# Attention's opening, the first expert's routing and the place of the second expert's counts in a kernel of attention and two MoE layers

## The chip, the cores and the metric

The kernel runs on one core of one Trainium2 chip. The metric is the device time of one execution in microseconds (us). TensorE (PE in the rows; PEld is its weight load), VectorE (DVE), ScalarE (ACT), GpSimd (POOL) and SyncE (SP, which issues most DMAs) each work off an instruction queue of their own, in order.

## What is computed

Attention with 4 sink positions and a window of 128, then an MoE layer in which each token goes to its best expert, then an MoE layer in which each expert takes at most 384 tokens, by the order of all logits.

```python
def _attn_ref(q, k, v, n_sink, window):             # (4, 8, 768, 64)
    scores = scale * np.matmul(q, k.transpose(0, 1, 3, 2))
    keep = is_sink | in_window                       # 4 sinks, window 128
    scores = np.where(keep, scores, -1000000000.0)
    a = np.exp(scores - np.max(scores, axis=-1, keepdims=True))
    a = a / (np.sum(a, axis=-1, keepdims=True) + 1e-09)
    return np.matmul(a, v).astype(np.float32)

def _moe_ref(x, modality_id, w_gate, modality_bias, w1, w2):   # x (3072, 512), 8 experts, 1024 hidden
    logits = x @ w_gate + modality_bias[modality_id]
    e_idx = np.argmax(logits, axis=1)
    ...
        h = np.maximum(x[mask] @ w1[e], 0.0)
        out[mask] = gate_w[mask, None] * (h @ w2[e])

def _moe2_ref(x, w_gate, w1, w2):
    cap = N // E                                     # 384
    flat = (x @ w_gate).flatten()
    for idx in np.argsort(-flat):
        tok, e = (int(idx) // E, int(idx) % E)
        if assigned[tok] >= 0 or counts[e] >= cap:
            continue
        assigned[tok] = e
        counts[e] += 1
    ...
        h = np.maximum(x[mask] @ w1[e], 0.0)
        out[mask] = h @ w2[e]
```

## The kernel before

**Attention** (0 to 200 us) goes through 48 groups `k` of two units each, three groups to a pair of heads. Each group's scores (`qk_mm`, L306) go through masks and maximum on VectorE (L317 to L325), the exponential on ScalarE (L335), a transpose on TensorE (L343), a copy on ScalarE (L348), a select on GpSimd (L354, L359) and the product with v (L378, a group later). The sinks have a path of their own: `sinkpack` (L387, L388, GpSimd), `sinktr` (L392), and `rows` (L411, L413), which multiplies with `bd`, a table that `init` (L257 to L285) builds in the first twenty steps from the sink values `vst` and `vsx` (both loaded), with dots `px<-wgp,vst` on TensorE (L264), their split into high and low part (`vsh`), and products into `bd` on ScalarE, GpSimd and VectorE. `warm` (L225) issues matmuls on zeros, 14 ahead of the loop and 7, 6, 5, 4, 3, 2 behind, which produce nothing. Other work (tables, routing of the first MoE, gathers of its first two tiles) stands in a list `bg`, of which the loop pops two steps a group.

**First MoE.** `Gate.after_batch` routes each of the four batches in steps `v1` to `v4` (L564 to L597); `v3b` (L588, L590) counts with matmuls of the one-hot table `oh`. Batch 2's steps are popped in the first FFN steps.

**FFN.** `Ffn.run` lists steps (an expert's quarter of the hidden width each). Each operand is split into a high and a low part, so a product is three matmuls: `ph<-xh/xl,w1h/w1l` (L930) and `y<-w2h/w2l,hh/hl` (L873). The low parts of the weights are made on VectorE or GpSimd (L845, L826). The rows of the next expert are gathered by GpSimd (L1744, three indirect DMAs of 128 rows), and `xprep` (L740 to L742) transposes them in four lots of 3 at fixed places in steps 6 and 7 of the expert ahead.

**Second MoE's routing** (`Route.steps`) finds each expert's threshold by iterations: a comparison `cmp` of 128x1792 on VectorE, thirteen count matmuls `rt<-OH,cmp` (L1560), two small operations, a matmul `rt<-gg,ones` (L1813), a maximum, and the next bound. After the last iteration `A` marks the expert's tokens, and `compact_steps` (L1387 to L1419) turns it into row numbers `idx`: a sum, a rank, and 28 matmuls `rc<-ft,ohb` (L1419). The first expert's iterations run with nothing beside them but `warm` (L749, by the numbers in `WT`); the others' run in between the FFN's matmuls. A planner's clock sets their place: a step is taken when the estimated clock of TensorE has reached the estimated end of VectorE's work plus a constant, `CM[0]`, `CM[1]`, `CM[2]` for the counts of the first, the second and all later experts (`yield clk.dve + CM[...]`).

Of the kernel before, what the change touches and what calls it, by code (L numbers as in the profile page):

```python
# [22 lines left out]
NSINK = 4  # L23
# [17 lines left out]
NSL = 128 * NSUB  # L41

C_ID, C_CAUS, C_M0, C_M1, C_TRI, C_IOTA, C_IW, C_BD, C_P = 0, 128, 256, 384, 512, 640, 768, 832, 840
C_W = 848


def host_consts():
# [24 lines left out]
def load_consts(nc, g, cpool, cst):  # L72
# [25 lines left out]
def late_consts(nc, g):  # L98
# [8 lines left out]
    def small():  # L107
        V.tensor_scalar(g.tcol[:, :, 0], g.iota[:, 0:NT], -1.0, float(NT - 1), op0=OP.mult, op1=OP.add)
        V.tensor_scalar(g.tcol[:, :, 1], bc(g.cst[:, C_P:C_P + 1], [128, NT]), -1.0, 128.0, op0=OP.mult, op1=OP.add)
        V.memset(g.tcr, 0.0)  # L110
# [5 lines left out]
        V.memset(g.o1, 1.0)  # L116
# [3 lines left out]
    return [small] + [(lambda t=t, c=c, o=o, w=w: fill(t, c, o, w))  # L120
                      for t, c, o, w in ((g.iob, 1.0, 0, 64), (g.iob, 1.0, 64, 64), (g.iou, 128.0, 0, 32), (g.iou, 128.0, 32, 32))]
# [62 lines left out]
def attention(ctx, tc, g, qT, kT, v4, vsT, vsR, wg, put_x, after_batch, bg, drain=True):  # L184
# [32 lines left out]
    load_pair(0)  # L217
    g.cst_load()
    load_pair(1)
    load_v(0)  # L220

    def warm(k):
        pz = ps.tile([128, 512], F32, name="po", bufs=2)
        for _ in range(k):
            nc.tensor.matmul(pz, g.wz[:, :128], g.wz, start=True, stop=True)  # L225

    warm(WARM)
    neg = one.tile([128, 128], F32, name="neg")
# [9 lines left out]
    nc.gpsimd.memset(rw[:, :, 128:144], 0.0)  # L238
    for s in range(2):
        o = slice(64 * s, 64 * s + 64)  # L240
        nc.sync.dma_start(rw[o, :, 128 + 8 * s:136 + 8 * s], wgv[o])
    bd = one.tile([96, B * NP, 2, 144], F32R, name="bd")
    psk = []
    for i in range(4):
        t = one.tile([128, 3, 8, NSINK], F32R, name=f"psk{i}")
        nc.gpsimd.memset(t.bitcast(F32), 0.0)
        psk.append(t)
    nc.gpsimd.memset(bd[:, 0:4].bitcast(F32), 0.0)
    vsh = wk.tile([96, B * NP, 72], F32, name="vsh", bufs=1)
    msk = one.tile([128, 3, 128], I32, name="msk")  # L250
    for c in (0, 2, 4):
        scale_q(0, c)
    for i, c in ((1, C_M0), (2, C_M1), (0, C_CAUS)):
        nc.vector.tensor_copy(msk[:, i, :], g.cst[:, c:c + 128])

    def init(n):
        V = nc.vector  # L257
        if n == 0:
            g.cst_derive()
            V.tensor_copy(rw[:, :, 0:128], bc(g.ident[:, None, :], [128, NP, 128]))  # L260
        if n in (2, 4):
            g.pw = ps.tile([96, B * NP, 8], F32, name="px")
        for p in {2: range(4), 4: range(4, 10), 5: range(10, 16)}.get(n, ()):
            nc.tensor.matmul(g.pw[:, p, :], vst[:, p, :], wgp[:, p % NP, :], start=True, stop=True)  # L264
        if n in (3, 6):
            r = slice(0, 4) if n == 3 else slice(4, 16)
            V.tensor_copy(vsx[:, r, 64:72], g.pw[:, r])
            V.tensor_copy(vsh[:, r].bitcast(F32R), vsx[:, r])
        if n in (4, 7):
            r = slice(0, 4) if n == 4 else slice(4, 16)  # L270
            V.tensor_tensor(vsh[64:96, r].bitcast(F32R), vsx[64:96, r], vsh[64:96, r], op=OP.subtract)
        k = n - 5 if n < 9 else (4 + (n - 9) // 2 if (n - 9) % 2 == 0 else 16)
        if 0 <= k < 16:
            c, m = divmod(k, 4)
            blk, hd = divmod(m, 2)
            mk = g.cst[:96, C_BD + m:C_BD + m + 1]
# [1829 lines left out]
```

## Time and profile before

| what | us |
|---|---|
| median of three runs (lowest, highest) | 882.87 (882.37, 883.36) |
| the profiled execution | 881.1 |
| its span, first to last instruction | 879.4 |
| attention | 0 to 200 |
| first MoE | 200 to 490 |
| its tail and the second MoE's first routing | 480 to 535 |
| second MoE's FFN, with the other experts' routing | 535 to 879 |

All rows below are of the profiled execution. Their times count from the start of the span. In a timeline row the first number is the start, the second the duration, then the engine, the line of the kernel, the operation, what it writes and reads, the shape and a count; in brackets the idle time of the engine ahead of it and what ended that. Neighbouring operations of a kind share a row.

### The profile page before, as it was taken

What the parts mean: (1) busy time and instruction counts of PE and PEld (TensorE: products, weight loads), DVE (VectorE), ACT (ScalarE), POOL (GpSimd) and SP (SyncE); (2) the same over time, 40 slices, a digit from 0 to 9 for tenths busy, and PEclk for the clock granted to TensorE, in tenths of its full rate; (3) what the DMA queues carried; (4) which work ended last, traced back from release to release, by engine and by line L of the source; (5) the groups of instructions that cost most, each with busy time, mean ns of one, the idle gap of its engine ahead of it and who ended that gap; (6) DMA issues with size and microseconds to landing.
All of it is one profiled execution on the core that took longest, in us unless ns stands there. A gap on an engine that the chain in (4) does not pass through costs nothing.

```text
span 879.4 us, 15309 instructions
## 1 busy us (share of the span) xinstructions
PE 835.4 (95%) x5071; PEld 664.3 (76%) x5071; DVE 597.0 (68%) x1737; ACT 387.1 (44%) x1093; POOL 354.9 (40%) x555
## 2 busy tenths in 40 slices
PE   8789999998999999999999987899999999999997
PEld 4556666676888888888888646788888878889996
DVE  3868787866659696969794467767778775753320
ACT  3677777764343434243342204243334333445431
POOL 2776757573420202010000006435464637375561
PEclk9999999999999999999999998998999999999999
DMA  8344555467463434444358133424435424336201
GB/s 252 111 144 144 138 157 150 101 220 285 56 190 108 154 118 157 130 156 133 108 156 279 64 104 130 153 78 145 166 122 181 161 91 142 119 134 226 96 37 40
DMA packets 69773, 123.90 MB, mean 141 GB/s; under 512 B 9651, under 2 KB 22453, under 8 KB 69558
## 3 DMA queue, kind: packets, MB, share of 16 engines
q1 hardware_dynamic: 62998, 103.41, 37.0%
q0 software_dynamic: 6688, 19.43, 7.0%
q8 instruction: 42, 0.69, 0.3%
q14 instruction: 45, 0.37, 0.2%
HBM read 103.11 MB, written 19.71 MB: 140 GB/s over the span
## 4 chain that ended last, share of the span: by engine, by line
PE 76%; DVE 9%; issue 5%; ACT 4%; POOL 2%; DMA 2%; SPq 1%; POOLq 0%; DVEq 0%; ACTq 0%
PE ph L930 27%; PE y L873 27%; PE sp L306 4%; PE po L378 3%; ACT P L335 2%; PE tr L740 2%; PE rt L1560 2%; PE pt L343 2%; PE px L413 1%; PE rc L1419 1%; DMA vsx<-in_vsR_dram 1%; DVE sc L150 1%; PE sp L392 1%; DMA xg<-xs,idx 1%; PE ph L1203 1%
## 5 line engine op out<-in xcount | busy, mean ns | idle before, releaser
L940 ACT ACTIVATE hh<-ph 128x384 fp32r<-128x384 f32 (+1 forms) x112 | 60.2, 538 | 276.7 <-PE ph L930 276.6
L930 PE MATMUL ph<-xh,w1h 128*128 128x384 f32 (+1 forms) x448 | 170.2, 380 | 0.0
L930 PE MATMUL ph<-xh,w1l 128*128 128x384 f32 (+1 forms) x448 | 162.5, 363 | 0.0
L930 PE MATMUL ph<-xl,w1h 128*128 128x384 f32 (+1 forms) x448 | 161.6, 363 | 0.0
L873 PE MATMUL y<-w2h,hh 128*128 128x512 f32 x384 | 155.8, 406 | 0.0
L873 PE MATMUL y<-w2h,hl 128*128 128x512 f32 x384 | 151.8, 395 | 0.0
L873 PE MATMUL y<-w2l,hh 128*128 128x512 f32 x384 | 151.7, 395 | 0.0
L941 DVE SCALAR_TENSOR_TENSOR hl<-ph,hh 128x384 fp32r<-128x384 f32 (+1 forms) x112 | 68.4, 611 | 113.8 <-ACT hh L940 112.5
L826 POOL TENSOR_TENSOR w2l<-w2r,w2h 128x512 fp32r<-128x512 f32 x64 | 89.0, 1399 | 63.9 <-ACT w2h L822 33.0
L1096 POOL DMA_INDIRECT xg<-xd,ent x26 | 29.3, 1126 | 190.1 <-DMA ent<-idtab 100.1
L1120 DVE SCALAR_TENSOR_TENSOR junk<-yr,wgb 128x512 f32<-128x512 f32 x160 | 103.0, 683 | 0.0
L930 PEld LDWEIGHTS ph<-xh,w1h 128*128 128x128 f32 x448 | 86.0, 192 | 10.0
L930 PEld LDWEIGHTS ph<-xh,w1l 128*128 128x128 f32 x448 | 85.7, 191 | 9.4
L930 PEld LDWEIGHTS ph<-xl,w1h 128*128 128x128 f32 x448 | 85.0, 190 | 7.8
L335 ACT ACTIVATE P<-sp,mx 128x132 f32<-128x132 f32 x192 | 69.2, 368 | 48.9 <-DVE mx L325 22.5
L873 PEld LDWEIGHTS y<-w2h,hl 128*128 128x128 f32 x384 | 72.9, 190 | 16.1
L873 PEld LDWEIGHTS y<-w2h,hh 128*128 128x128 f32 x384 | 73.3, 191 | 11.5
L873 PEld LDWEIGHTS y<-w2l,hh 128*128 128x128 f32 x384 | 73.1, 190 | 11.4
L306 PE MATMUL sp<-kr,qs 64*128 64x260 f32 (+1 forms) x384 | 58.4, 401 | 16.4 <-ACT P L335 16.3
L840 ACT ACTIVATE w1h<-w1r 128x512 fp32r<-128x512 f32 x112 | 69.7, 623 | 5.7 <-DMA w1r<-in_w_dram 3.4
L822 ACT ACTIVATE w2h<-w2r 128x512 fp32r<-128x512 f32 x112 | 69.6, 624 | 0.5 <-DMA w2r<-in_w_dram 0.5
L845 DVE TENSOR_TENSOR w1l<-w1r,w1h 128x512 fp32r<-128x512 f32 x80 | 63.4, 793 | 3.5 <-ACT w1h L840 3.5
(359 smaller groups left out, 1394.0 us busy)
## 6 DMA issues: line engine op xcount, KB each, us to landing
w1r<-in_w_dram SPq DMA_DIRECT2D x30, 1024.0 KB, 5.7
w2r<-in_w_dram SPq DMA_DIRECT2D x30, 1024.0 KB, 7.2
kr<-in_kT_dram SPq DMA_DIRECT2D x16, 396.0 KB, 4.5
qr<-in_qT_dram SPq DMA_DIRECT2D x16, 384.0 KB, 3.3
vr<-in_v_dram SPq DMA_DIRECT2D x16, 384.0 KB, 4.9
xd<-xb SPq DMA_DIRECT2D x16, 384.0 KB, 4.4
xs<-yr SPq DMA_DIRECT2D x24, 256.0 KB, 5.3
wgb<-in_wg2T_dram SPq DMA_DIRECT2D x1, 2048.0 KB, 12.0
```

The source lines that it names most:

```text
L306: nc.tensor.matmul(sp[:, hd, c0:260], qs[o:o + 64, 128 * i:128 * i + 128], kr[o:o + 64, k0:k0 + 260 - c0], start=True, stop=True)
L335: nc.scalar.activation(z.P[:, n % 2, hd, :], s.sp[:, hd, 128:260], AF.Exp, bias=s.mx[:, hd:hd + 1], accum_out=z.sm[:, n % 2, hd:hd + 1])
L822: nc.scalar.activation(ch[1][c][0], r[:, q, :], AF.Copy)
L826: eng.tensor_tensor(lo, r[:, q, :], h.bitcast(F32), op=OP.subtract)
L840: nc.scalar.activation(h, v, AF.Copy)
L845: eng.tensor_tensor(lo, v, h.bitcast(F32), op=OP.subtract)
L873: nc.tensor.matmul(o, l, r, start=(first and i == 0), stop=(end and i == 2))
L930: nc.tensor.matmul(ph, wp[:, c, :], xp_[:, c, 0:NTK], start=(d == 0 and i == 0), stop=(d == 3 and i == len(cut[d]) - 1))
L940: nc.scalar.activation(hh, ph, AF.Relu)
L941: nc.vector.scalar_tensor_tensor(hl, ph, 0.0, hh.bitcast(F32), op0=OP.max, op1=OP.subtract)
L1096: self.nc.gpsimd.indirect_dma_start(out=self.xg[j][:, a, :], out_offset=None, in_=self.G.xd[0:k, :], in_offset=bass.IndirectOffsetOnAxis(a ...
L1120: nc.vector.scalar_tensor_tensor(junk, yr[:, 0:DM], 1.0, wgb[:, e, :], op0=OP.mult, op1=OP.mult, accum_out=lg[:, e:e + 1])
```

## The change

**Opening.** The first pair's q and k are loaded in two pieces; the table of constants shrinks from 848 to 272 columns, as masks and the triangle are made on GpSimd and VectorE; `vst` is no longer loaded but built on GpSimd from a small table; `vsx` is loaded for four heads first, the other twelve behind the second pair; 9 warming matmuls stand ahead of the loop, and 7, 4, 3, 2 in the first four groups, behind the transposes; the sink dots go in fours to groups 1, 4, 6 and 8; the products into `bd` go to groups 2, 3 and every second group from 8 on; `bg` is popped from group 2 on; the clearing of `bd` goes.

**First MoE.** Only its first tile is gathered in attention's background; batch 2's steps are popped in attention's last groups, and its `v3b` gets the place rule that batch 3's had.

**Second MoE.** For the first expert the bound comes from a table `T` with one fused operation, and the comparison is split, 8 of 14 columns first, so that counts can start; `A` is made ahead of `cj` and `em`; `WT[2]` and `WT[3]` become 0 and 1 for the first expert (6 and 3 for the others, as before); a gather of 2 rows into the first expert's tile is issued at the start (`prime`); the first expert's transposes go block by block (`xfirst`). `CM[1]` goes from 0.7 to 2.0.

```diff
-WARM, WARM1 = 14, 8
+JC, NIT, FEW, IDLE = 64, 4, 2, (1, 2, 1)
+WARM, WARM1, WA = 9, 8, (7, 4, 3, 2)
-CM = 0.2, 0.7, 1.3
+CM = 0.2, 2.0, 1.3
-WT = 5, 2, 6, 3, 6, 2, 3, 16, 0, 2
+WT = 5, 2, (0, 6), (1, 3), 6, 2, 3, 16, 0, 2
...
+    raw[0] = wk.tile([128, S], F32, name="qr"), wk.tile([128, KW], F32, name="kr", bufs=3)
+    for qc, kc in ((slice(0, 256), slice(0, 2 * SEG)), (slice(256, S), slice(2 * SEG, KW))):
+        nc.sync.dma_start(raw[0][0][:, qc], qT[0, 0][:, qc])
+        nc.sync.dma_start(raw[0][1][:, kc], kT[0, 0][:, kc])
...
-    nc.sync.dma_start(vst, vsT)
-    nc.sync.dma_start(vsx[:, :, 0:64], vsR)
+    nc.sync.dma_start(vsx[:, 0:4, 0:64], vsR[:, 0:4])
+    load_v(0)
+    load_pair(1)
+    nc.sync.dma_start(vsx[:, 4:16, 0:64], vsR[:, 4:16])
+    P.memset(vst, 0.0)
...
+            P.tensor_scalar(v[:, :, a, s].rearrange("p (b z) s -> p b z s", z=3),
+                            bc(vsc[o, :, None, :], [64, B * NP, 3, NSINK]), 1.0, 1.0, op0=OP.mult, op1=OP.mult)
+    VC = {1: (0,), 4: (1,), 6: (2,), 8: (3,)}
...
-        v = [v1, v1b, v2, v2b, v3] + ([(RW, v3b)] if b == B - 1 else [nop, v3b]) + [v4]
+        v = [v1, v1b, v2, v2b, v3] + ([(RW, v3b)] if b > BE else [nop, v3b]) + [v4]
...
+        for a in range(A):
+            for d in range(4):
+                nc.tensor.transpose(p[d][:, 128 * a:128 * a + 128], xg[:, a, 128 * d:128 * d + 128], self.g.ident)
...
+                    if k == 0:
+                        if it > first:
+                            V.scalar_tensor_tensor(self.ub, bc(dd[:, 2, it - 1:it], [128, NR]), J, self.T, op0=OP.mult, op1=OP.add)
+                            self.against(V)
...
+                            V.tensor_scalar(self.T, S_, b1, dd[:, 1, it + 1:it + 2], op0=OP.subtract, op1=OP.mult)
...
-                    self.count(pn, range(HT + 1))
+                    self.count(pn, range(HT + 1), k == 0 and it > first)
```

TensorE in attention's opening, before: the sink dots of six heads stand between the scores of two groups.

```order
L306 MATMUL sp<-kr,qs 128x260 x2
L264 MATMUL px<-wgp,vst 96x8 x6
L343 MATMUL pt<-cst,P 128x128 x4
L378 MATMUL po<-lu,vr 64x256 x2
L306 MATMUL sp<-kr,qs 128x132 x2
L306 MATMUL sp<-kr,qs 128x260 x2
L392 MATMUL sp<-cst,psk_170 96x128
```

The same engine after the change, in group 1:

```order
L322 MATMUL sp<-kr,qs 128x260 x4
L359 MATMUL pt<-cst,P 128x128 x4
L273 MATMUL sp<-wgp,vst 96x8 x4
L220 LDWEIGHTS wz
L220 MATMUL px<-wz 128x512
```

The dots moved behind the transposes, four heads at a time, and into the bank of the scores.

TensorE at the seam of attention and the first MoE, before, where the last row matmuls are followed by the first transposes:

```order
L411 MATMUL px<-bd,skT 128x288
L413 MATMUL px<-rw,oT 128x144 x2
L740 MATMUL tr<-cst,xg 128x128 x4
L740 MATMUL ph<-cst,xg 128x128 x4
L740 MATMUL y_3258<-cst,xg 128x128 x4
```

After:

```order
L427 MATMUL px<-bd,skT 128x288
L429 MATMUL px<-rw,oT 128x144 x2
L615 LDWEIGHTS tri
L615 MATMUL px<-oh,tri 128x48
L617 LDWEIGHTS ones
L617 MATMUL px<-oh,ones 128x48
```

Batch 2's counts (one matmul with `tri`, six with `ones`) moved from the first FFN step to right behind the last rows; five more count matmuls and then the transposes follow.

TensorE in the second MoE, before, from the last of expert 1's 28 compaction matmuls (21 FFN matmuls stand between it and the first transposes `tr<-cst,xg`):

```order
L1419 MATMUL rc<-ft,ohb 128x12
L930 MATMUL ph<-xh,w1h 128x384
L930 MATMUL ph<-xh,w1l 128x384
L930 MATMUL ph<-xl,w1h 128x384
L1532 MATMUL rt<-d_6824,of 128x2
L930 MATMUL ph<-xh,w1h 128x384
```

After:

```order
L1464 MATMUL rc<-ft,ohb 128x12
L767 MATMUL tr<-cst,xg_6986 128x128 x3
L976 MATMUL ph<-xh,w1h 128x384
L976 MATMUL ph<-xh,w1l 128x384
L976 MATMUL ph<-xl,w1h 128x384
```

The compaction moved 21 FFN matmuls back, and the transposes kept their place. In the same way 27 matmuls between expert 2's compaction and its transposes have become 9, and 51 for expert 3 have become 27; a count stands there for both, before and after.

## Rows read from the trace of the kernel before

**Rows 1.** The page's first part: busy us, share of span, instructions.

```profile
PE 835.4 (95%) x5071; PEld 664.3 (76%) x5071; DVE 597.0 (68%) x1737; ACT 387.1 (44%) x1093; POOL 354.9 (40%) x555
```

**Rows 2.** The chain of work that ended last, share of the span by engine.

```profile
PE 76%; DVE 9%; issue 5%; ACT 4%; POOL 2%; DMA 2%; SPq 1%; POOLq 0%; DVEq 0%; ACTq 0%
```

**Rows 3.** Timeline of TensorE in attention: opening, groups 4, 8 and 47.

```profile
1.41 7.36 PE L225 MATMUL po<-wz 128*128 128x512 bf16 x21 [1.41 <-POOL wz L80]
8.70 0.49 PE L306 MATMUL sp<-kr,qs 64*128 64x132 f32 x4
...
27.80 0.71 PE L306 MATMUL sp<-kr,qs 64*128 64x260 f32 x4 [1.72 <-ACT P L335]
...
44.74 1.15 PE L306 MATMUL sp<-kr,qs 64*128 64x260 f32 x8
...
189.02 1.15 PE L306 MATMUL sp<-kr,qs 64*128 64x260 f32 x8
```

**Rows 4.** The chain in order of time, opening: start, us, what.

```profile
5.75 9.84 DMA vsx<-in_vsR_dram
```

**Rows 5.** Busy time by engine, granted clock, DMA share, GB/s, first window.

```profile
0.00:10.00 10.00, 8.59 (x30) 3.29 (x30) 1.72 (x8) 2.73 (x5) 3.61 (x16) 1.00 0.79 269
```

**Rows 6.** Timeline of TensorE behind the seam, first MoE's first FFN step.

```profile
211.90 0.20 PE L588 MATMUL rt<-oh,tri 128*128 128x48 bf16 x1 [2.43 <-DVE oh L579]
...
212.69 0.63 PE L930 MATMUL ph<-xh,w1l 128*128 128x512 f32 x1
...
215.61 0.39 PE L930 MATMUL ph<-xh,w1h 128*128 128x512 f32 x1
```

**Rows 7.** Timeline of VectorE and TensorE, first expert's third iteration.

```profile
512.34 0.35 DVE L150 SCALAR_TENSOR_TENSOR sc<-J8m,dd,sc 128x1 f32<-128x1 f32 x2
...
512.93 1.09 DVE L150 TENSOR_TENSOR cmp<-ub,iou 128x1792 bf16<-128x1792 bf16 x1
...
514.08 0.96 PE L1560 MATMUL rt<-OH,cmp 128*128 128x16 bf16 x13 [1.00 <-DVE cmp L150]
...
515.59 2.74 PE L749 MATMUL y<-wz 128*128 128x512 bf16 x6
...
517.02 0.25 DVE L150 SCALAR_TENSOR_TENSOR A<-S__76,sc,oe 128x28 bf16<-128x28 f32 x1
```

**Rows 8.** Timeline of GpSimd and TensorE, first expert's rows.

```profile
528.28 1.78 POOL L1744 DMA_INDIRECT xg<-xs,idx  x1 [0.31 <-issue]
...
532.56 0.48 PE L740 MATMUL tr<-cst,xg 128*128 128x128 f32 x1 [1.28 <-DMA xg<-xs,idx]
```

**Rows 9.** Timeline of VectorE and TensorE, an iteration of expert 1.

```profile
539.68 1.95 DVE L150 SCALAR_TENSOR_TENSOR sc<-J8m,dd,sc 128x1 f32<-128x1 f32 x2
...
542.95 2.10 DVE L150 TENSOR_TENSOR cmp<-ub,iou 128x1792 bf16<-128x1792 bf16 x1
...
545.10 0.95 PE L1560 MATMUL rt<-OH,cmp 128*128 128x16 bf16 x13 [2.20 <-DVE cmp L150]
```

**Rows 10.** Expert 1: timeline of compaction, third gather, transposes; then a window.

```profile
560.69 1.86 PE L1419 MATMUL rc<-ft,ohb 128*128 128x12 bf16 x28
...
566.07 0.96 POOL L1744 DMA_INDIRECT xg<-xs,idx  x1 [0.30 <-issue]
...
568.39 0.33 PE L740 MATMUL tr<-cst,xg 128*128 128x128 f32 x1 [0.96 <-DMA xg<-xs,idx]
569.88 0.41 PE L740 MATMUL tr<-cst,xg 128*128 128x128 f32 x1 [1.16 <-DMA xg<-xs,idx]
...
570.00:574.00 4.00, 4.00 (x15) 3.55 (x16) 1.56 (x3) 1.61 (x4) 0.60 (x1) 0.57 0.94 333
```

**Rows 11.** Expert 2: timeline of compaction, third gather and first transposes.

```profile
607.40 1.84 PE L1419 MATMUL rc<-ft,ohb 128*128 128x12 bf16 x28
...
614.54 0.94 POOL L1744 DMA_INDIRECT xg<-xs,idx  x1 [0.30 <-issue]
...
619.25 0.49 PE L740 MATMUL tr<-cst,xg 128*128 128x128 f32 x3
```

More of the change, by code (lines that the diff above doesn't have):

```diff
@@ L109, in small, with rows @@
         V.tensor_scalar(g.tcol[:, :, 1], bc(g.cst[:, C_P:C_P + 1], [128, NT]), -1.0, 128.0, op0=OP.mult, op1=OP.add)
+        V.memset(g.o1, 1.0)
+    def rows():
         V.memset(g.tcr, 0.0)
@@ L256, in init @@
[L256 to L259, printed above, removed]
-            V.tensor_copy(rw[:, :, 0:128], bc(g.ident[:, None, :], [128, NP, 128]))
[L261 to L267, printed above, removed]
+    V.tensor_copy(msk, bc(caus[:, None, :], [128, 3, 128]))
@@ new lines, in attention @@
+    V.tensor_copy(msk[:, 1, 0:4], g.ones[:, 0:4])
+    V.tensor_copy(msk[:, 2, 0:4], g.wz[:, 0:4])
+    V.tensor_copy(g.tri, caus)
+    scale_q(0, 0)
+    for s in range(2):
+        o = slice(64 * s, 64 * s + 64)
+        v = vst[o].rearrange("p b (z a c s) -> p (b z) a c s", z=3, c=2, s=NSINK)
+        for a in range(2):
+            P.tensor_scalar(v[:, :, a, s].rearrange("p (b z) s -> p b z s", z=3),
+                            bc(vsc[o, :, None, :], [64, B * NP, 3, NSINK]), 1.0, 1.0, op0=OP.mult, op1=OP.mult)
@@ L1012, in ereg2, with idle, pop @@
         return self.ereg(j)
-    def idle(self):
+    def idle(self, i):
         pass
-    pop = idle
+    def pop(self):
+        pass
 class Src1(Src):
@@ L1555, in compare, with against, count @@
                         bc(self.g.iou[:, None, :, sl], [128, A, JC, w]), op=OP.is_ge)
-    def count(self, pn, tiles):
+    def against(self, V):
+        ub = fold(self.ub)
+        for i, (o, e) in enumerate(self.cuts):
+            shape = [128, 2, JC, e - o]
+            V.tensor_tensor(self.cmp2[i], bc(ub[:, :, None, o:e], shape), bc(self.g.iou[:, None, :, o:e], shape), op=OP.is_ge)
+    def count(self, pn, tiles, parts=False):
         for t in tiles:
-            self.nc.tensor.matmul(pn, self.cmp[:, :, :, t].rearrange("p a j -> p (a j)"), fold(self.OH)[:, :, t, :],
+            c = self.cmp2[t // HA][:, :, :, t % HA] if parts else self.cmp[:, :, :, t]
+            self.nc.tensor.matmul(pn, c.rearrange("p a j -> p (a j)"), fold(self.OH)[:, :, t, :],
                                   start=(t == tiles[0]), stop=(t == tiles[-1]), skip_group_check=True)
@@ L1696, in pop, with prime, idle @@
                 f()
-    def idle(self):
-        for i in range(IDLE):
+    def prime(self):
+        nc = self.nc
+        z = self.p.tile([2, 1], I32, name="zi")
+        nc.gpsimd.memset(z, 0)
+        self.x[0] = self.xp.tile([128, 3, DM], F32, name="xg2", bufs=2)
+        nc.gpsimd.indirect_dma_start(out=self.x[0][0:2, 0, :], out_offset=None, in_=self.xs,
+                                     in_offset=bass.IndirectOffsetOnAxis(ap=z, axis=0))
+    def idle(self, i):
+        for _ in range(IDLE[i]):
             self.pop_main()
-            if i == EM:
-                self.nc.vector.tensor_copy(self.em2, self.e[0])
-        self.warm = None
+        if i == 1:
+            self.nc.vector.tensor_copy(self.em2, self.e[0])
+            self.warm = None
     def fill(self, k):
@@ L1781, in steps @@
         dn = None
+        self.cuts = ((0, HA), (HA, HT + 1))
+        self.cmp2 = [self.xp.tile([128, 2, JC, e - o], BF, name=f"cmp{o}", bufs=1) for o, e in self.cuts]
         for k in range(E):
@@ L1873, in moe2 @@
         rt.ps, rt.xp, rt.warm = f.ps, f.wk, f.warm
+        rt.prime()
         puts = []
```

203 lines of the change are left out of this document (121 added, 82 removed).

## Prediction

> **What bounds the kernel now.** The page's first part is read first: TensorE is busy 95% of the span and no other engine comes near [rows 1]. The chain that ended last says the same in its own way, TensorE 76% and VectorE 9% [rows 2]. So the matmuls themselves are the bound over most of the span, and the change, which keeps the number of FFN matmuls, can only win where TensorE idles, runs warming matmuls, or runs at its lower clock. Four such places are touched: the first 45 us of attention, the seam between attention and the first MoE (212 us), the second MoE's routing of its first expert (507 to 533 us), and the places of the second and third experts' compaction and transposes (550 to 620 us). Each was read in the order of time on TensorE, with VectorE and GpSimd beside it.
>
> **Opening.** TensorE runs 21 warming matmuls in 7.36 us from 1.41; only then, at 8.70, come the first scores; group 8 of the 48 begins at 44.74, group 47 at 189.02 [rows 3]. From group 8 on a group takes (189.02 - 44.74)/39 = 3.70 us; the first eight took 36.04, so 6.4 us more than eight steady ones. That excess has names: the chain of this stretch waits 9.84 us for the load of vsx [rows 4], a score matmul waits 1.72 us for the exponential [rows 3], and the sink dots come in lumps of six heads. The change leaves 9 warming matmuls. At the rate of the row they take 3.2 us, at the lower clock level (512 columns at 1.2 GHz, 0.43 us each) 3.8; I take the latter, so the first scores start near 5.1. The loads must keep up: by the second pair's first group (near 16 us) two pairs of q and k, one v and the small tables, some 2.4 MB by the shapes in the diff, have to be in; at the 269 GB/s of the first window [rows 5] that is 9 us, so loading is not the bound. The sink dots, casts and products do not vanish; they go in fours to groups 1, 4, 6 and 8, on engines that the steady groups leave room on. With eight steady groups, group 8 starts at 5.1 + 8 x 3.70 = 34.7: **-10.0 us**. The ends: if only the first start moves and the old pace stays, -3.6; with a pace of 3.55 (the fastest stretch I would grant), -11.2. I take -10.0, since most named causes of the excess are gone from the path. The cover is GpSimd's: it now builds the sink values (one memset, four products) ahead of its first select, and if that is late the third group waits.
>
> **The seam.** At 211.90 TensorE stands 2.43 us for VectorE's one-hot of batch 2, and comes back at its lower level: 0.63 us a matmul against 0.39 a little later, six of them, pitch 0.43 against 0.23, so 1.2 us more [rows 6]. In the new order batch 2's routing steps stand between the last groups' outputs on VectorE, and its counts on TensorE right behind the last row matmuls. That takes away 3.6 us. It adds some ten short VectorE operations (about 2 us) in groups where the next output waits for VectorE, and the seven count matmuls with two dependent operations, ahead of the first transposes; behind the count on TensorE's queue wait these transposes and with them the whole first FFN. I price this at 1.3. Net **-2.3**, between -3.6 and 0. Moving tile 1's gathers of the first MoE into its run I cost at nothing: they land many steps ahead of use; uncovered it would be one gather, some 4 us.
>
> **The first expert's routing, to the landing of its rows.** An iteration before: two small products (0.35), the comparison over all 1792 elements (1.09), a wait of 1.00 on TensorE, then thirteen count matmuls [rows 7]. Now one fused operation takes the place of two plus one (-0.26 from start to start), and the count begins after 1024 elements, 1.09 x 1024/1792 = 0.62; the eight first tiles (0.59) cover the second half. So -0.7 an iteration, two of them, less 0.25 for a table operation that VectorE runs in between: -1.15. A no longer stands behind three small operations: -0.3. Six warming matmuls, from 515.59 to 518.33, stood ahead of A's matmul, while A was ready at 517.27 [rows 7]: -1.0; two of three later ones, -0.4. The early two-row gather on GpSimd should spare the late start of the gathers: the third takes 1.78 us against 0.96 for the usual one [rows 8, 10]: -0.6. Sum **-3.4**, between -2.5 and -4. The third block then lands at 529.1 and not at 532.5, where TensorE waited 1.28 for it [rows 8]. The transposes by blocks gain little, as the copies behind them keep their pace.
>
> **Behind it: compaction against gathers.** This is where something comes back. Expert 1's rows are gathered after the compaction matmuls (ends 562.55), and the first transposes need all three blocks: the third gather starts at 566.07, and the third transpose at 569.88 [rows 10]. So 7.3 us pass from the last compaction matmul, and between lie 21 FFN matmuls; TensorE waited 0.96 + 1.16 = 2.1 us [rows 10]. In the new order the compaction stands 21 FFN matmuls later, right ahead of the transposes, with none in between: the wait is about 7.0 us, **+4.9**. Part of it may be no loss: if the counts ahead, now later on TensorE, no longer wait (2.20 us before, [rows 9]) TensorE reaches this place sooner. I allow 1.4 for that, so **+3.5**, between 0 and +6. (By the Trainium skill, DMA: Bandwidth & Descriptors, section on the anatomy of one DMA by the GpSimd path, such a transfer takes about 2.0 us plus its bytes at 436 GB/s, so an estimated 2.6 for one block; the row has 3.8 from issue to use, and that decides here. By the page this wait and the next would be 1.2 shorter each, and the sum 2.4 lower.) Expert 2: compaction ends at 609.2, the third gather starts at 614.54 and the first transposes come at 619.25 without a wait [rows 11], with 27 FFN matmuls and a count between. The landing follows the third issue by 3.8, so at 618.3, 9.1 after the compaction; with an idle VectorE it would be 7.3, as for expert 1. In the new order 9 FFN matmuls (2.1 us) and one count (1.0) lie between: a new wait of 4.2 to 6.0, of which a count's wait may cover some; **+4**. Expert 3: 51 become 27, 6.2 us and a count, so 0 to 2, **+0.5**. After expert 1's wait TensorE's granted clock was 0.57 for four microseconds [rows 10]; as longer waits and shorter ones seem to lead to the same, I take that as unchanged for expert 1, and as part of the range for expert 2. Sum **+8**, between 0 and +12.
>
> **The sum.** -10.0 - 2.3 - 3.4 + 8.0 = -7.7. The profiled run took 881.1 (span 879.4 and 1.7 around it), 1.8 below the median of 882.87; so 873.4 for such a run and **875** as a median.
>
> **Rivals.**
> *No price behind (A).* TensorE reaches expert 1's compaction so much sooner that its wait replaces waits for counts, and expert 2's rows land in time since VectorE is free earlier. For it: the 2.20 us before a count and the lower clock behind it would go. Against: nothing stands between compaction and transposes any more. The last term is then near +0.5: 867.
> *The opening keeps its pace (B).* The warming goes, but the exponentials, selects and small VectorE pieces still set about 4.3 us a group; -5 in place of -10: 880. For it: VectorE gets the masks and all the sink casts, GpSimd the sink values. Against: the long load and the lumps are off the path.
> *VectorE beside GpSimd (C).* Expert 1's iterations run in the stretch in which GpSimd makes low parts of weights: there two small products took 1.95 us and a comparison 2.10, against 0.35 and 1.09 [rows 7, 9]. The change moves one more iteration there, 3.9 us longer, and only 21 matmuls (4.8 us) lie between counts: some 3 us more, 878. (The Trainium skill, SBUF — State Buffer, section on who interferes with whom, says that a VectorE instruction with two inputs in SBUF and a GpSimd instruction that reads SBUF block one another for a whole instruction; the trace's lengthening by about 1.0 agrees. By that rule this rival is the likelier the more of the weights is still left to GpSimd.)
> *Slower (D).* Each gather wait is a full one and each is followed by a stretch at the lower clock, which then costs some 2 to 3 us each: 7 + 3, 6 + 3 and 2 + 3 for experts 1 to 3, with 2.1 and one such stretch taken off, is +19; against -15.7 that gives 886. It decides as soon as the last term is over 15.7.
>
> **Chances.** Forecast (873 to 878) 0.45, A 0.2, B 0.13, C 0.1, D 0.12. The range of 8 in 10 reaches from A's lower side, with the opening at its better end, to between B and D: 866 to 883; the forecast's own is 871 to 879. About 0.2% (1.8 us) is what a measurement of this kernel can tell from none: faster is below 881.1, slower above 884.6. A, the forecast, C and most of B are faster: 0.82; the seam between B and D is the same: 0.07; slower 0.11.
>
> **What would show it.** Right: group 0's scores near 5 and group 8's near 35; no wait for the one-hot at the seam; the first expert's third block landing some 16 us after the start of its third count, in place of 18.4 (514.08 to 532.5); behind expert 1's compaction a wait for its gather of about 7 us, and one of about 4 behind expert 2's. Wrong: scores of group 8 at 40 or later; transposes of experts 1 and 2 that wait for nothing; waits for comparisons that grow in their place.

## The result, and the profile after

The kernel after takes **891.1 us** (median of 6 runs, 888.4 to 892.5); the kernel before, in 6 runs beside it, 883.1 (882.3 to 885.4). The ratio is 1.0095, 95% interval 1.0067 to 1.0122: slower by about 8 us, where 875 was forecast, and outside the range of 866 to 883. The profiled run of after took 891.1 with a span of 889.4, 10.0 more than the span of before; 2.0 of these come from the profiled run of before (881.1), which lay that much under the 883.1.

The page of after, busy time by engine and the chain that ended last by engine; [rows 1, 2] are their counterparts:

```profile
PE 835.0 (94%) x5042; PEld 664.2 (75%) x5047; DVE 608.0 (68%) x1759; ACT 386.0 (43%) x1091; POOL 347.3 (39%) x559
PE 70%; DVE 12%; issue 6%; DMA 4%; ACT 4%; POOL 3%; POOLq 0%; SPq 0%; DVEq 0%; ACTq 0%
```

TensorE does as much work as before (835.0 us), but its part of the chain fell from 76% to 70%, and VectorE's and the DMAs' grew. So TensorE waits more. Where it waits is found by cutting the span at marks that both kernels have: the last group's scores, the first count of the second MoE, its first FFN matmul, and the last matmul.

| stretch | before | after | change | predicted |
|---|---|---|---|---|
| start to the last scores | 189.02 | 183.68 | -5.3 | -10.0 |
| last scores to the first count | 317.80 | 318.98 | +1.2 | -2.3 |
| first count to the first FFN matmul | 27.79 | 24.22 | -3.6 | -3.4 |
| first FFN matmul to the last matmul | 338.44 | 356.33 | **+17.9** | +8.0 |

The four changes add up to +10.2, where -7.7 was predicted; the tails of the two spans behind the last matmul differ by 0.2. The fourth row decides. Busy time by engine in that stretch, the kernel before first (columns: us, busy us and count of TensorE, its weight loads, VectorE, ScalarE, GpSimd, then granted clock, DMA share, GB/s):

```profile
534.61:873.05 338.44, 329.81 (x1957) 283.98 (x1955) 204.47 (x516) 131.55 (x289) 182.47 (x170) 0.98 0.37 124
```

and of the kernel after:

```profile
526.88:883.21 356.33, 332.94 (x1955) 286.08 (x1955) 209.89 (x524) 131.59 (x290) 178.07 (x170) 0.97 0.36 121
```

The matmuls are the same ones. Before, TensorE stood 338.44 - 329.81 = 8.6 us of it; after, 23.4. So **14.8 us are new waits**, and 3.1 are the same matmuls at a lower granted clock. What it waited for from the first FFN matmul on (us in total, times, the longest), kernel before:

```profile
PE tr L740 <- DVE xl L742: 3.1, 3, 1.7
PE rt L1560 <- DVE cmp L150: 2.8, 2, 2.2
PE tr L740 <- DMA xg<-xs,idx: 2.1, 2, 1.2
```

and the kernel after:

```profile
PE tr L767 <- DMA xg<-xs,idx: 12.3, 7, 4.4
PE rc L1437 <- DVE tb L144: 3.8, 2, 2.2
PE rt L1621 <- DVE cmp L144: 3.5, 2, 2.5
PE ph L976 <- DVE hl L987: 1.2, 1, 1.2
PE tr L767 <- DVE xl L769: 0.9, 1, 0.9
```

The waits for gathered rows grew by 10.2. Here they are on TensorE's timeline, expert 1's three, expert 2's three, and expert 3's; they answer to [rows 10, 11]:

```profile
561.82 1.80 PE L1464 MATMUL rc<-ft,ohb 128*128 128x12 bf16 x28 [0.28 <-ACT ckj L1824]
568.00 0.48 PE L767 MATMUL tr<-cst,xg 128*128 128x128 f32 x1 [4.38 <-DMA xg<-xs,idx]
569.47 0.47 PE L767 MATMUL tr<-cst,xg 128*128 128x128 f32 x1 [0.99 <-DMA xg<-xs,idx]
571.03 0.47 PE L767 MATMUL tr<-cst,xg 128*128 128x128 f32 x1 [1.09 <-DMA xg<-xs,idx]
...
621.66 0.30 PE L767 MATMUL tr<-cst,xg 128*128 128x128 f32 x1 [1.96 <-DMA xg<-xs,idx]
623.08 0.33 PE L767 MATMUL tr<-cst,xg 128*128 128x128 f32 x1 [1.12 <-DMA xg<-xs,idx]
624.30 0.48 PE L767 MATMUL tr<-cst,xg 128*128 128x128 f32 x1 [0.89 <-DMA xg<-xs,idx]
...
673.12 0.33 PE L767 MATMUL tr<-cst,xg 128*128 128x128 f32 x1 [1.86 <-DMA xg<-xs,idx]
```

Expert 1: 4.38 + 0.99 + 1.09 = 6.5 us; from the end of the compaction (563.6) to the third transpose 7.4 pass, as before (7.3), but no FFN matmul lies in between. Expert 2: 4.0. Expert 3: 1.9. Behind expert 1's wait the granted clock was at its lower level (0.50, 1.2 GHz) for eight microseconds, where [rows 10] have 0.57 for four:

```profile
568.00:572.00 4.00, 1.92 (x6) 1.33 (x7) 0.00 (x0) 0.46 (x1) 1.49 (x3) 0.50 0.74 194
572.00:576.00 4.00, 4.00 (x13) 3.42 (x12) 1.20 (x3) 1.66 (x5) 1.29 (x1) 0.50 0.99 352
```

A second place is one that the prediction had only as a rival (C, VectorE beside GpSimd): an iteration of expert 1 that now runs inside the FFN. VectorE's timeline of after:

```profile
528.73 0.16 DVE L144 MAX8 J8m<-rt 128x8 f32<-128x8 f32 x1
528.93 2.22 DVE L144 SCALAR_TENSOR_TENSOR sc<-J8m,dd,sc 128x1 f32<-128x1 f32 x2
531.07 1.36 DVE L144 TENSOR_SCALAR ub<-S__77,sc,dd 128x28 bf16<-128x28 f32 x1
532.46 2.10 DVE L144 TENSOR_TENSOR cmp<-ub,iou 128x1792 bf16<-128x1792 bf16 x1
```

and TensorE's, for the same iteration:

```profile
526.56 0.18 PE L1898 MATMUL rt<-gg,ones 64*128 64x8 bf16 x1
...
534.61 0.95 PE L1621 MATMUL rt<-OH,cmp 128*128 128x16 bf16 x13 [2.49 <-DVE cmp L144]
536.78 0.69 PE L976 MATMUL ph<-xh,w1h 128*128 128x384 f32 x1 [1.21 <-DVE hl L987]
```

The operand `gg` of the matmul at 526.56 was ready at 524.97, but the matmul stands on TensorE's queue behind the first expert's twelve transposes (524.95 to 526.63, the last four at the third gathered block's landing, 525.97). Its maximum then came only at 528.73, behind the low parts `xl` on VectorE (526.86 to 528.81), and the iteration ran while GpSimd was busy without a gap from 528.58 on: the two small operations took 2.22 where [rows 7] have 0.35, the comparison 2.10 in place of 1.09. The count waited 2.49 for it, the FFN behind it 1.21. (The Trainium skill, SBUF — State Buffer, section on who interferes with whom, has a VectorE instruction with two SBUF inputs and a GpSimd instruction that reads SBUF block one another; these rows agree in kind, [rows 9] too.)

### The profile page after: what moved, and what is told of

Same layout as the page of the kernel before. It is cut to its first block, busy times and chain, and to the rows that moved or that the text cites. A ratio compares the mean times of both kernels' runs of the same rounds, so it can differ in the third digit from the quotient of the medians.

```text
span 889.4 us, 15273 instructions
## 1 busy us (share of the span) xinstructions
PE 835.0 (94%) x5042; PEld 664.2 (75%) x5047; DVE 608.0 (68%) x1759; ACT 386.0 (43%) x1091; POOL 347.3 (39%) x559
## 4 chain that ended last, share of the span: by engine, by line
PE 70%; DVE 12%; issue 6%; DMA 4%; ACT 4%; POOL 3%; POOLq 0%; SPq 0%; DVEq 0%; ACTq 0%
PE ph L976 24%; PE y L914 24%; PE sp L322 4%; PE po L394 3%; ACT P L351 2%; PE tr L767 2%; PE rt L1621 2%; DVE sc L144 2%; DMA xg<-xs,idx 1%; PE pt L359 1%; PE px L429 1%; PE y L790 1%; DVE mx L341 1%; DMA idtab<-entry,slot 1%; PE rc L1464 1%
## 5 line engine op out<-in xcount | busy, mean ns | idle before, releaser
L867 POOL TENSOR_TENSOR w2l<-w2r,w2h 128x512 fp32r<-128x512 f32 x64 | 86.1, 1351 | 71.6 <-ACT w2h L863 46.8
L976 PEld LDWEIGHTS ph<-xh,w1l 128*128 128x128 f32 x448 | 85.6, 191 | 10.6 <-POOL w1l L886 0.7
L886 POOL TENSOR_TENSOR w1l<-w1r,w1h 128x512 fp32r<-128x512 f32 x32 | 44.1, 1377 | 58.7 <-ACT w1h L881 58.7
```

The costliest lines, as they stand in the source:

```text
L867: eng.tensor_tensor(lo, r[:, q, :], h.bitcast(F32), op=OP.subtract)
L886: eng.tensor_tensor(lo, v, h.bitcast(F32), op=OP.subtract)
L976: nc.tensor.matmul(ph, wp[:, c, :], xp_[:, c, 0:NTK], start=(d == 0 and i == 0), stop=(d == 3 and i == len(cut[d]) - 1))
```

## The experiments

Two numbers place this work: `CM[1]`, which sets how late expert 1's and 2's steps come (0.7 before, 2.0 after), and `IDLE`, which says how many of expert 1's first steps stand beside the first weights, ahead of the first expert's transposes and behind them (1, 2 and 1; in the kernel before all four stand ahead of the transposes). Theory: the loss is made by these two, the rest of the change gains. Rivals: the opening, the seam, or one of the new operations loses it. Each experiment's ratio is to the kernel before, run beside it, whose median lay between 882.5 and 883.5.

**e1: after with the old `CM[1]`.**

```diff
-CM = 0.2, 2.0, 1.3
+CM = 0.2, 0.7, 1.3
```

> The changed kernel with CM[1] back at 0.7 and nothing else. In the order, expert 1's compaction then stands 15 FFN matmuls ahead of the first transposes (0 in the changed kernel, 21 before), expert 2's 27 (9), expert 3's 51 (27). Theory 1: the 17.7 us that the second MoE's FFN loses are the waits for gathers of experts 1 to 3 (12.3 us) with the low clock and the waits for A and tb around them, all from the later counts. Then this runs 13 to 17 us under the changed kernel, 874 to 878, with gather waits of some 4 us at expert 1 and none at 2 and 3. Theory 2: the loss is VectorE beside GpSimd in the first FFN steps (the waits of 2.49 for a comparison and 1.21 for hl), which the split iterations bring at any CM. Then it stays above 885.

Measured: 880.3 (879.0 to 886.9), ratio to before 0.9971 [0.9935, 1.0007]: 10.8 under after. What TensorE waited for from the first FFN matmul on, in e1:

```profile
PE tr L767 <- DMA xg<-xs,idx: 4.4, 4, 2.0
PE rt L1621 <- DVE cmp L144: 4.3, 2, 4.0
PE tr L767 <- DVE xl L769: 3.4, 3, 1.7
```

The gathers' waits fell from 12.3 to 4.4, as the theory says, and the stretch from the first FFN matmul to the last took 343.4 in place of 356.3. But one count now waits 4.0 us by itself (at 535.18), and 343.4 is still 4.9 over before. The gain of 10.8 is short of the 13 to 17 that theory 1 asked for, and the time is below the 885 of theory 2: `CM[1]` is the larger part, not all.

**e2: before with the new `CM[1]`.** The same line the other way round, on the kernel before.

```diff
-CM = 0.2, 0.7, 1.3
+CM = 0.2, 2.0, 1.3
```

> The kernel before with CM[1] at 2.0 and nothing else: expert 1's compaction 6 FFN matmuls ahead of the transposes, expert 2's 9, expert 3's 27. Theory 1: this constant alone costs what the second MoE lost: 9 to 15 us over the kernel before, 892 to 898, with waits of about 5, 4 and 2 us behind the three compactions. Theory 2: within 4 us of the kernel before.

Measured: 890.4 (888.8 to 893.7), ratio 1.0084 [1.0057, 1.0111], so 7.7 over before, a little under what was expected. The gathers' waits in the same stretch of e2:

```profile
PE tr L740 <- DMA xg<-xs,idx: 9.8, 8, 2.4
```

They rose from 2.1 to 9.8, without any other part of the change; the profiled stretch took 348.8 in place of 338.4. With e1 this settles the cause of the larger part from both sides.

**e3: after, with the preparation of the next expert's rows later in the FFN.** If the only fault is that the transposes come too early for the gathers, moving the transposes must help as well.

```diff
-        f.run(list(range(E)), w1, w2, rt, yout, hook=rt.pop, xp=((6, 0), (6, 2), (7, 0), (7, 2)))
+        f.run(list(range(E)), w1, w2, rt, yout, hook=rt.pop, xp=((6, 2), (7, 0), (7, 1), (7, 2)))
```

> The changed kernel (CM[1] 2.0), the second MoE's transposes at later places: 123, 135, 141, 144 FFN matmuls into an expert and not 114, 123, 135, 144. The order shows that expert 1's compaction moves with them (again none between), while those of experts 2 and 3 go back to 255 and 399, 36 and 60 ahead of their transposes. Theory 1: expert 1's wait of about 6.5 stays, the 4.0 and 1.9 of experts 2 and 3 go, with the low clock behind them: 6 to 9 us under the changed kernel, 882 to 885. Theory 2: within 2 us of the changed kernel.

Measured: 891.4 (889.7 to 893.8), ratio 1.0095 [1.0062, 1.0128]: nothing gained; the expectation failed. The waits in e3, same stretch:

```profile
PE tr L767 <- DMA xg<-xs,idx: 7.3, 3, 5.3
PE tr L767 <- DVE xl L769: 6.8, 12, 1.3
```

Experts 2 and 3 no longer wait for gathers, but expert 1's wait is 7.3 all the same (the compaction moved with it), and transposes closer together wait for the low parts `xl` on VectorE, 6.8 against 0.9.

**e4: after with the first MoE's gathers and batch 2's counts as before.** A test of the seam.

```diff
-        v = [v1, v1b, v2, v2b, v3] + ([(RW, v3b)] if b > BE else [nop, v3b]) + [v4]
+        v = [v1, v1b, v2, v2b, v3] + ([(RW, v3b)] if b == B - 1 else [nop, v3b]) + [v4]
...
-        fs = [lambda: self.xids(j), nop, nop, nop, lambda: self.xtile(j), nop]
-        for a in range(self.width(j)):
-            fs += [lambda a=a: self.gather(j, a), nop]
-        return fs + [w]
+        fs = []
+        for j in range(NE):
+            fs += [lambda j=j: self.xids(j), nop, nop, nop, lambda j=j: self.xtile(j), nop]
+            for a in range(self.width(j)):
+                fs += [lambda j=j, a=a: self.gather(j, a), nop]
+        return fs[:16] + [w] + fs[16:]
```

> The changed kernel with both tiles of the first MoE gathered in attention's background again, so that batch 2's routing falls into the first FFN steps, as before. The second MoE is untouched. If my price of the seam was right (2.3 gained by the move), this is 2 us slower than the changed kernel. If the move only shifts the loss (1.9 us more in the last groups, 2.3 more up to the first FFN matmul, 3.6 no longer lost behind it), it is within 1.5 us of it, with the last row matmuls some 2 us earlier and the wait of 2.4 for the one-hot back.

Measured: 892.5 (891.4 to 894.0), ratio 1.0102 [1.0062, 1.0142], 1.4 over after, which the spread of the runs can't tell from nothing. TensorE's timeline of after at the seam:

```profile
196.91 0.20 PE L615 MATMUL px<-oh,tri 128*128 128x48 bf16 x1 [0.62 <-DVE lp L447]
196.95 0.29 PE L617 MATMUL px<-oh,ones 128*128 128x48 bf16 x6
197.79 1.09 PE L767 MATMUL tr<-cst,xg 128*128 128x128 f32 x4 [0.55 <-PE px L617]
...
202.58 0.58 PE L976 MATMUL ph<-xh,w1h 128*128 128x512 f32 x1
```

and of e4:

```profile
196.62 0.63 PE L767 MATMUL tr<-cst,xg 128*128 128x128 f32 x4 [0.66 <-PE px L429]
...
199.93 0.58 PE L976 MATMUL ph<-xh,w1h 128*128 128x512 f32 x1
...
208.20 0.18 PE L615 MATMUL rt<-oh,tri 128*128 128x48 bf16 x1 [2.44 <-DVE oh L606]
...
208.69 0.40 PE L976 MATMUL ph<-xh,w1l 128*128 128x512 f32 x1
```

The wait for the one-hot is back in e4 (2.44), without the lower clock behind it that [rows 6] have: 0.40 us a matmul, not 0.63. After pays elsewhere: its transposes run at the lower clock (1.09 for four, 0.63 in e4; granted clock 0.55 from 197.7 to 201.2), behind two waits (0.62 and 0.55), and the first FFN matmul comes 6.3 us after the last row matmuls in place of 4.0. From the last scores to the second MoE's first count e4 is shorter by 2.2 in its profile (316.8 and 319.0). The other profiles agree: the stretch took 316.8 and 317.8 in the two kernels that have the old seam besides (e2 and before), and 317.7 to 320.1 in the nine with the new one. Over its runs e4 is not faster. In its profile the 2.2 are lost again in stretches with a lower granted clock: 1.6 in attention (0.91 between 20 and 60 us, 1.00 in after), 2.8 from the first FFN matmul on (0.96 and 0.97). So the runs alone can't tell a small gain of the seam from a small loss; the profiles point to a loss of some 1 to 2 us, and none shows the gain of 2.3.

**e5: e1, and the first expert's transposes behind three of expert 1's steps.** In after, one, two and one step stood at the three places; the third place is behind the transposes.

```diff
-JC, NIT, FEW, IDLE = 64, 4, 2, (1, 2, 1)
+JC, NIT, FEW, IDLE = 64, 4, 2, (1, 3, 0)
-CM = 0.2, 2.0, 1.3
+CM = 0.2, 0.7, 1.3
```

> The kernel of e1 (the change with CM[1] at 0.7) with IDLE (1, 3, 0) and not (1, 2, 1): all of expert 1's second iteration is again issued ahead of the first expert's transposes, as in the kernel before, and the compactions stand 21, 27 and 51 matmuls ahead, as there. Theory: what e1 did not give back comes from the last idle step, which put the matmul of gg behind the transposes, which wait for a gather; so the two small products and the comparison run beside GpSimd's weights (2.2, 1.4, 2.1 in place of 0.35, 0.3, 1.1), and a count waits 4.0. Then this is 3 to 5 us faster than e1: 875 to 877, that count's wait is under 0.5, and the one of 2.2 of the kernel before is back at the third iteration. Rival: GpSimd slows whichever iteration comes there, and the waits only move: within 1.5 us of e1.

Measured: **875.05** (871.5 to 880.2), ratio 0.9908 [0.9874, 0.9942]: 5.2 under e1, a little more than expected, 16 under after, and 7.4 under before. TensorE in e5:

```profile
526.09 0.18 PE L1898 MATMUL rt<-gg,ones 64*128 64x8 bf16 x1
...
528.82 0.96 PE L1621 MATMUL rt<-OH,cmp 128*128 128x16 bf16 x13
...
538.68 0.95 PE L1621 MATMUL rt<-OH,cmp 128*128 128x16 bf16 x13 [2.68 <-DVE cmp L144]
```

The matmul of expert 1's iteration comes ahead of all twelve transposes (the first is at 526.20), its two small products take 0.35 again and its comparison 1.09, the count that waited 4.0 in e1 waits for nothing (at 528.82), and the next one's wait (2.68) is of the size of before's (2.20). The profiled execution took 880.2, 5 us over e5's median, so its stretches are not set beside those of e1; under e10, e6 stands for it, the same kernel but for a two-row gather, with the same median.

**e10: after with the new `IDLE` alone**, the fourth corner of the square.

```diff
-JC, NIT, FEW, IDLE = 64, 4, 2, (1, 2, 1)
+JC, NIT, FEW, IDLE = 64, 4, 2, (1, 3, 0)
```

> The changed kernel with IDLE (1, 3, 0) and CM[1] left at 2.0: compactions 6, 9 and 27 matmuls ahead of the transposes. With the changed kernel (891.1), e1 (880.3) and e5 (875.1) this fills the square of the two constants. If the two losses are independent, 891.1 - 5.2 = 886, with waits for gathers of about 5, 4 and 2 us. If the iteration behind the transposes costs only where the counts are early, within 1.5 us of the changed kernel.

Measured: 886.5 (883.1 to 888.6), ratio 1.0031 [1.0005, 1.0058], as expected if the two losses are independent. Most of the gathers' waits stay, in e10 from the first FFN matmul on:

```profile
PE tr L767 <- DMA xg<-xs,idx: 10.1, 7, 2.6
```

| median, us | `CM[1]` 2.0 | `CM[1]` 0.7 | difference |
|---|---|---|---|
| `IDLE` (1, 2, 1) | 891.1 (after) | 880.3 (e1) | 10.8 |
| `IDLE` (1, 3, 0) | 886.5 (e10) | 875.05 (e5) | 11.4 |
| difference | 4.6 | 5.2 | |

The two numbers act apart from one another: about 11 and about 5 us. Both together are 16, and lead from after to e5, 7.4 under the kernel before measured beside it (882.5). That is what the rest of the change is worth; its three upper rows in the table of stretches, -5.3 + 1.2 - 3.6, add up to -7.7.

What the 5 us of `IDLE` consist of, the waits show only in part. From after to e10 the gathers' waits fall by 2.2 (12.3 to 10.1), since the compaction stands 6 FFN matmuls ahead of the transposes and not 0, those for comparisons by 2.0 (3.5 to 1.5) and for `hl` by 0.8 (1.2 to 0.4). From e1 to e6 the gathers' fall by 2.4 (4.4 to 2.0) and those for `tb` by 1.1 (1.7 to 0.6), but those for comparisons only by 0.5 (4.3 to 3.8). So about half is again the distance from compaction to transposes, and e5's theory, by which all of it was the iteration beside GpSimd's weights, is borne out only in part: with the early counts that wait moves to the next iteration, as its rival said. Why the compaction waits for `tb` (3.8 in after, 2.5 in e2, 4.2 in e10, none in before) no run shows.

**e6: e5 without the early two-row gather.**

```diff
-        rt.prime()
```

> The kernel of e5 without the early gather of two rows. The changed kernel's first split comparison waits 0.99 for that gather to land. If that wait and the gain at the third gather (0.95 for 1.78, and 0.3 after idx for 0.9) cancel, this is within 1 us of e5: count 2 about 1 us earlier, first gather 0.6 later after idx, third one 0.8 longer. If the gather was worth the 0.6 I gave it, 0.6 to 1 slower.

Measured: 875.0 (873.0 to 877.8), ratio 0.9928 [0.9894, 0.9962]; no difference from e5. The question was the first split comparison, which starts 0.99 late in after, with the early gather named as what it waited for. VectorE's timeline of after:

```profile
505.78 1.17 DVE L144 TENSOR_TENSOR cmp<-ub,iou 128x1024 bf16<-128x1024 bf16 x2 [0.99 <-DMA xg<-xs,zi]
```

and of e6, where that gather does not exist:

```profile
507.72 1.17 DVE L144 TENSOR_TENSOR cmp<-ub,iou 128x1024 bf16<-128x1024 bf16 x2 [0.99 <-DVE ub L144]
```

The same 0.99 stands there. So the gather was not the cause. The third gather of the first expert took 1.71 on GpSimd without it and 0.95 with it, as the prediction had it; the 0.6 that the prediction gave it doesn't show in the time.

**e9: e5 with the split comparison in the old comparison's tile.** If the 0.99 belongs to the first write into newly made tiles, it leaves the comparison here.

```diff
-        self.cmp2 = [self.xp.tile([128, 2, JC, e - o], BF, name=f"cmp{o}", bufs=1) for o, e in self.cuts]
+        flat, at = self.cmp.rearrange("p a j t -> p (a j t)"), 0
+        self.cmp2 = []
+        for o, e in self.cuts:
+            w = 2 * JC * (e - o)
+            self.cmp2.append(flat[:, at:at + w].rearrange("p (a j t) -> p a j t", a=2, j=JC))
+            at += w
```

> The kernel of e5 with the split comparison written into the tile that the unsplit one has (the same columns, in two regions), in place of two new tiles in the pool that is opened for the second MoE. e6 showed the 0.99 us ahead of the first split comparison without the early gather too, so the gather is not its cause. In the order, that comparison is the first instruction to write into the new pool, and waits for every engine and DMA queue; in the kernel before a small memset of z was the first, and stood idle 0.68. Theory: the 0.99 goes from the comparison to z, behind which less is queued: the second count starts 1 us earlier against the first, the third 0.5 to 1 us, and the run is 0.5 to 1 us under e5. Rival: the time is the fused operation's or the comparison's own, and stays.

Measured: 878.2 (872.0 to 881.5, 12 runs), ratio 0.9938 [0.9913, 0.9964]; 0.5 to 1 under e5 was expected, and there is no gain over it. VectorE's timeline of e9:

```profile
508.13 1.17 DVE L144 TENSOR_TENSOR cmp<-ub,iou 128x1024 bf16<-128x1024 bf16 x2
510.61 0.09 DVE L144 MEMSET z<- 128x32 uint32 x1 [0.59 <-issue]
```

The comparison now follows `ub` at once (507.85), and a wait of 0.59 stands before the clearing of `z`, the next first write of a new tile of that part, where before has 0.68 as well. That it is the first write into newly made tiles is what both experiments agree with; what exactly it waits for is not shown. From the first count to the start of the compaction e9 is 0.7 shorter than e5, which its time does not show: in its profile the first count already came 2.3 later than e5's, 1.5 of it in attention, which the experiment doesn't touch (granted clock 0.91 between 20 and 60 us, 0.96 in e5).

**e7: e5 with a still smaller `CM[1]`**, 0.4 in place of 0.7 (the same line).

> The kernel of e5 with CM[1] at 0.4: expert 1's compaction 24 matmuls ahead of the transposes (21 in e5), the third iteration's count 3 matmuls earlier. Theory 1 (each FFN matmul between compaction and transposes takes 0.23 off the gather's wait): 0.7 less waiting there, but the count waits 0.7 more; so within 1 us of e5.

Measured: 875.6 (871.7 to 877.5), ratio 0.9913 [0.9885, 0.9942]. The waits change their owners (expert 1 waits for no gather, a count waits 3.4, expert 2 waits 2.3 for a gather) and the sum stays. 0.4 and 0.7 are alike; 2.0 is far out.

**e8: e5 with 14 warming matmuls ahead of the first scores in place of 9.**

```diff
-WARM, WARM1, WA = 9, 8, (7, 4, 3, 2)
+WARM, WARM1, WA = 14, 8, (7, 4, 3, 2)
```

> The kernel of e5 with 14 warming matmuls ahead of attention's loop and not 9. If TensorE's queue sets the opening (as my sum had it), the first scores start 1.6 to 2.1 us later and the whole run is that much longer: 1.5 to 2 us over e5. If the opening is paced by VectorE, ScalarE and the loads behind it, the later groups catch up and it is within 0.7 us of e5.

Measured: 877.3 (875.0 to 882.2), ratio 0.9952 [0.9926, 0.9978], 2.2 over e5. TensorE's timeline of e8:

```profile
1.28 5.80 PE L220 MATMUL po<-wz 128*128 128x512 bf16 x14 [1.28 <-DVE wz L76]
7.02 0.93 PE L322 MATMUL sp<-kr,qs 64*128 64x132 f32 x8
...
186.50 1.15 PE L322 MATMUL sp<-kr,qs 64*128 64x260 f32 x8
```

The first scores move by 2.2 (4.83 in e5), the last ones by 2.1 (184.44), the median by 2.2. From the first scores to the last 179.5 us pass in e8, and 179.6 in e5: nothing is caught up. So TensorE's queue sets the start of the scores, and what is put on it ahead of them is paid to the end.

## Why the prediction was wrong, step by step

The sum was off by 17.9: 9.9 behind the routing, 4.7 in the opening, 3.5 at the seam, -0.2 in the first expert's routing.

**Behind the routing: gathers right, all that goes with them wrong by 9.9.** The largest failure is here. The prediction saw the waits for the gathers coming (about 7 for expert 1, about 4 for expert 2, 0 to 2 for expert 3) and they came: 6.5, 4.0, 1.9. With the 2.1 of before taken off it priced them at +9.4, and they measured +10.2. The step that failed is the next one. The sum took 1.4 off for counts that would wait less, and put the lower clock at nothing. Instead the other waits grew by 4.6 (14.8 less 10.2): 3.8 for `tb` and 1.2 for `hl` are new, those for comparisons rose by 0.7, those for `xl` fell by 2.2, and the rest are small ones. And the lower clock cost 3.1. That is 0.8 + 1.4 + 4.6 + 3.1 = 9.9.

The number behind most of it is `CM[1]`: e1, and e5 beside e10, put 11 us on it in the changed kernel, e2 7.7 in the kernel before. The prediction had read its effect in the order of the matmuls. `IDLE` (5 us) was not treated by itself. About half of its effect, the last 6 matmuls between expert 1's compaction and the transposes, was in the term for expert 1; the iteration beside GpSimd was in rival C and not in the sum, and the matmul with `gg` that put it there, behind the transposes, was not named.

The remaining part of that stretch was priced by the row with the usual wait: 3.8 us from a gather's issue to its use. After has 567.14 to 571.03, 3.9. (By the Trainium skill, DMA: Bandwidth & Descriptors, section on the anatomy of one DMA by the GpSimd path, the estimate was 2.6; the rows read here don't agree with it, and the measured one was the right choice.)

**The opening: -5.3 and not -10.0.** The first scores came at 5.24, as said. Then the rest of the term failed. Busy time by engine from the first scores to group 8's, in after, and from there to the last scores:

```profile
5.24:37.21 31.97, 28.93 (x221) 18.15 (x221) 25.49 (x80) 20.17 (x87) 14.59 (x45) 1.00 0.60 188
...
37.21:183.68 146.47, 134.45 (x1143) 93.92 (x1141) 118.31 (x425) 108.61 (x473) 102.20 (x264) 1.00 0.49 138
```

The first eight groups take 4.0 us each and not the steady 3.70. TensorE is busy 28.9 of these 32.0 us: 16 warming matmuls and 24 matmuls of sink dots stand in them, and the prediction gave the groups the pace of groups that have neither. e8 shows what a matmul on that queue costs ahead of the scores; that fewer in the groups would gain was not tried. From group 8 on 39 groups take 146.5 where they took 144.3 (189.02 - 44.74): 1.5 of it is TensorE's own work (0.8 are eight matmuls of sink dots that have moved there), 0.7 more waiting, while VectorE has 7.1 us more to do. In numbers: -3.5 at the start, -4.1 in the first eight groups, +2.2 behind. Rival B's -5 came out as a number, but not as B had it: at 4.3 us a group, group 8 would start near 39.5 and the rest would keep its pace. It started at 37.2, and 2.2 were lost behind it, where neither the forecast nor B had a price.

**The seam: +1.2 and not -2.3.** The wait is gone, as said, and from the first FFN matmul to the second MoE's first count 3.1 is gained, where 3.6 was said. But batch 2's steps in attention's last groups cost 2.0 there (last scores to last rows 12.6 in place of 10.6), and the counts ahead of the transposes 2.3 more, with TensorE's granted clock at 0.55 in the transposes behind them. The addition was priced at 1.3 and measured 4.3. In e4 the removed wait costs 2.44 without a lower clock behind it, so the 1.2 that [rows 6] had for the clock was no fixed part of that wait.

**The first expert's routing: right in sum, in part by luck.** Predicted -3.4, measured -3.6; but the -3.4 was said of the way to the third block's landing, and that took 23.3 from the first count (502.66 to 525.97), before 25.7 (506.82 to 532.56): -2.4. The other 1.1 comes behind the landing, where the first FFN matmul now follows the third block by 0.9 in place of 2.1, with the transposes by blocks, of which the prediction said that they gain little. By parts, in TensorE's timeline of after:

```profile
509.58 0.87 PE L1621 MATMUL rt<-OH,cmp 128*128 128x16 bf16 x13 [0.55 <-DVE cmp L144]
...
525.97 0.33 PE L780 MATMUL tr<-cst,xg 128*128 128x128 f32 x1
```

From the third count to the landing 16.4 us pass, predicted some 16, before 18.5: right. The third count follows the second in 3.05 in place of 3.69, as said; the second follows the first later (3.87, before 3.57), by the 0.99 ahead of the first split comparison, which was not foreseen. So the two iterations gave 0.3 and not 1.15.

**The rivals.** Slower (D) was priced at 886, from +19 behind and full gains elsewhere; it was to decide "as soon as the last term is over 15.7". The last term came out at 17.9, and the gains at 7.7 and not 15.7. B's -5 and D's +19 put together give 881.1 - 5 - 2.3 - 3.4 + 19 = 889.4 for the profiled run, which took 891.1. That is close by luck: the seam is 3.5 too low in it and D 1.1 too high, and D came to its 19 by longer gather waits (+12.9, measured +10.2) and more lower clock (+6, measured +3.1), without the other waits (+4.6). VectorE beside GpSimd (C), priced at 3, came true in one iteration of after, with 2.49 + 1.21 of waits, of which 2.8 went with the new `IDLE` (e10); no price behind (A) did not. The range took the rivals one at a time, and so ended at 883. And the forecast of 875 is what the change gives when its two numbers are set otherwise (e5), which is no merit of the sum, since its terms were not these.

## What to carry to other kernels

A step that is moved later on an in-order engine is costed from what follows it: here 7.4 us from compaction to the last gathered block, and FFN matmuls taken out from between show up as a wait of about their length. With 21, 15, 6 and 0 of them between expert 1's compaction and transposes the waits were 2.1, 3.7, 4.4 and 6.5 (before, e1, e2, after), 0.21 a matmul on average. Where an opening's extra work is spread over steady steps, count it on the engine that sets the pace, before that pace is used for them. Rivals that touch different stretches can both come true, so the range has to hold their sum.

## What the hardware showed that was not expected

- A wait's price is not its length alone, and not the same in each run. Expert 1's 6.5 us of waits stood ahead of eight microseconds at 0.50; the 2.44 at e4's seam stood ahead of none. Runs of one kernel differ with the clock, though not by it alone: e5 took 871.5 at a mean granted clock of 0.986 and 880.2 at 0.976, but 877.3 at 0.974.
- The same attention (in e4 with more gathers beside it) can have a stretch at a lower clock in one execution and none in another. Between 20 and 60 us the granted clock was 1.00 in after and e10, 0.96 in e1, e3, e5 and e7, 0.91 in e4, e6 and e9; the last scores came at 183.1 to 183.7, 184.4 to 184.5 and 185.3 to 185.9. A stage's difference of 2 us between two profiles is therefore read with their clocks beside it (before had 1.00 there too, so the -5.3 of the opening stands).
- A first write into newly made tiles waited 0.99 (after, e5, e6) or 0.59 to 0.68 (before, e9), and the traces don't show for what; in after the trace named a gather, whose removal left the wait as it was.
